# Staging the cosine chain in four slots, and spreading the token sums and splits over six pairs

## The chip, the cores and the metric

The kernel runs on one core of one Trainium2 chip. The metric is the device time of one execution in microseconds, from the first to the last of its work; the median of the runs shown is compared. TensorE is written PE here, VectorE DVE, ScalarE ACT, SyncE SP (it only issues DMAs), as in the profile.

## The reference, cut to what matters

An attention through 32 packed queries gives x (4608 tokens by 512). Two MLPs follow:

```python
def _moe_ref(x, w_gate, w_val, w_out):
    g = x @ w_gate
    silu = g * (1.0 / (1.0 + np.exp(-g)))
    return (silu * (x @ w_val)) @ w_out          # d_ff 1536

def _moe2_ref(x, w_in, w_out):                   # x: 4608 x 512
    h = x @ w_in                                 # 4608 x 2048
    g = h * np.cos(h)
    return g @ w_out                             # 4608 x 512
```

Everything is float32. The change concerns the second MLP alone: its h, its h*cos(h), and the preparation of its tokens.

## The kernel before, in words

The first half of the kernel (attention and first MLP, eight batches) writes its result to a DRAM scratch tensor. The second half, from line 625, is the second MLP. Every float32 operand of a matmul is kept as a pair (hi, lo) of float32r values, made by `split` (lines 85 to 87): ACT copies with rounding to hi, DVE subtracts to give lo. A product then takes three matmuls (hi*hi, hi*lo, lo*hi).

The second MLP works on 6 chunks of 768 tokens. In a chunk there are 8 pairs (`q`, 0 to 7; over the kernel `p`, 0 to 47), a pair being two blocks of 128 hidden features. One pair multiplies a 2x2 block of weights by a 2x2 block of tokens in Winograd's way, with seven products instead of eight. Product 0 to product 6 (`product`, lines 672 to 682) take six matmuls each into four PSUM banks A, Bk, Ck, Dk (lines 738 to 777); product 4 accumulates into A, product 5 into Ck, product 6 into Dk. Around them ACT copies A to SBUF (line 748, called p1 below), and DVE makes v = p1 + Bk, u3 = v + Ck, c22 = u3 + Dk, and later c21 and c12. c22, A, c21 and c12 are the four tiles of h of the pair (128 x 384 each).

Between the products stand up to three `down` products (lines 684 to 711), twelve matmuls of 512 columns each, that multiply finished tiles of earlier pairs by w_out. `step_down` releases those of group j (pairs 2j and 2j+1) from pair 2j+3 on, three per pair; so pairs 0 to 2 have none, and ten follow the last pair. Each result is copied or added to an SBUF accumulator by `evict`, run from the list `post`.

`chain` (lines 655 to 670) makes h*cos(h) and its split for one tile h: ACT t = h/2pi + 1/4 (line 657), ACT k = integer of t (659), DVE t = t - k (662), ACT sine of t (663), DVE t = t*h (667), ACT hi copy (86), DVE lo (87). The order of all instructions is the order in which the program issues them, and each engine takes its own in that order. The multiplication of a tile is put off to the next `chain` call (`late_mul`), the split to the one after (`late_split`), so that on ACT a call is t, k, hi copy of the tile two before, sine.

The second kind of work is the tokens of the next chunk. `load_x2` (513 to 518) loads four tiles from DRAM scratch in pair q = 3; `sums_x2` (526 to 529) makes four differences, two each at the start of q = 5 and q = 6; `split_x2` (531 to 534) splits the seven right-hand sides, all in q = 7, at seven places called by `swap_x` (742 to 744): before product 0, before v, before u3, before c22, before product 5, before product 6 and after the third of the four `chain` calls. The weights of pair p+2 are loaded by SP as the products of pair p are issued (`load_up`, fourteen buffers, 256 KB each), those for `down` two groups ahead (`load_wd`, 512 KB each). PSUM has eight banks; a pair uses four for its products and three for its downs, and each bank is handed out in the order in which banks come free. A tile gets its buffer when it is first written.

Of the kernel before, what the change touches and what calls it, by code (L numbers as in the profile page):

```python
# [10 lines left out]
F32 = mybir.dt.float32  # L11
F32R = mybir.dt.float32r
U32 = mybir.dt.uint32
I32 = mybir.dt.int32
U8 = mybir.dt.uint8
AF = mybir.ActivationFunctionType
ALU = mybir.AluOpType
# [9 lines left out]
TH = 384  # L27
NCH = NT // (2 * TH)
NPF = NF2 // 2
NG = NPF // 2  # L30
SBUFS, CBUFS = 11, 18
SIN_SCALE = 6.28318500518798828

PI = float(np.pi)
TWO_PI = 2.0 * float(np.pi)
# [5 lines left out]
def attention_mlp_kernel(ctx: ExitStack, tc: tile.TileContext, qT, kT, vP, pP, wgv, w1o, w2, out):  # L41
    nc = tc.nc
    PE, ACT, DVE, SP = nc.tensor, nc.scalar, nc.vector, nc.sync
# [37 lines left out]
    quarter = cst.tile([128, 1], F32, name="quarter")  # L81
# [3 lines left out]
    def split(src, hi, lo, eng=DVE):  # L85
        ACT.activation(out=hi, in_=src, func=AF.Copy)  # L86
        eng.tensor_tensor(out=lo, in0=src, in1=hi.bitcast(F32), op=ALU.subtract)  # L87
# [96 lines left out]
    def a_t(b):  # L184
        for r in range(2):
            e = E.pop(r)
            ET[r] = []
            for c0, n in ((0, 3), (3, 2)):
                tp = bank([128, n, 128], "tp")
                for c in range(n):  # L190
                    o = 128 * (c0 + c)
                    PE.transpose(out=tp[:, c, :], in_=e[:, o:o + 128], identity=ident)
                et = mt([128, n, 128], F32, "ET")
                ACT.activation(out=et, in_=tp, func=AF.Copy)
                ET[r].append(et)
# [20 lines left out]
    def a_ppt(b):  # L216
        for r in range(2):
            tp = bank([128, 128], "ppt")
            PE.transpose(out=tp, in_=ppu.pop(r).rearrange("p i d -> p (i d)"), identity=ident)
            ppT[b, r] = st.tile([128, 128], F32, tag="ppT", name="ppT", bufs=4)  # L220
            ACT.activation(out=ppT[b, r], in_=tp, func=AF.Copy)
# [76 lines left out]
    def flush_wo():  # L298
        while wo_wait:
            a, i, w_ = wo_wait.pop(0)  # L300
            wo[a, i] = wt([128, 2, 4, 128], F32R, "wo")
            split(w_, wo[a, i][:, 0].rearrange("p f o -> p (f o)"), wo[a, i][:, 1].rearrange("p f o -> p (f o)"))
# [10 lines left out]
    def w2_load(i):  # L313
        if i < 4 * NF2:
            w2_raw[i] = raw_words(mt, w2[i // 2, :, 256 * (i % 2):256 * (i % 2) + 256], 256)
# [44 lines left out]
    def w2_store():  # L360
        while w2_done:
            p, dst = w2_done.pop(0)
            SP.dma_start(out=dst, in_=p.bitcast(F32))
# [34 lines left out]
    def flush_split():  # L398
        while pend_split:
            pend_split.pop(0)()  # L400
# [100 lines left out]
    late = {}  # L501
# [9 lines left out]
    xb, xs = {}, {}  # L511
# [8 lines left out]
    def sum_x2(key, x, y):  # L520
        xb[key] = xt([128, 2, TH], F32, "xt")
        DVE.tensor_tensor(out=xb[key], in0=xb[x], in1=xb[y], op=ALU.subtract)

    RIGHT = ((0, 0), "t2", "t3", "t1", (1, 0), "t4", (1, 1))

    def sums_x2(n):
        sum_x2(*(("t1", (0, 1), (0, 0)), ("t2", (1, 1), "t1"), ("t3", (1, 1), (0, 1)), ("t4", (1, 0), "t2"))[n])
        if n == 2:
            del xb[0, 1]

    def split_x2(n):
        x = late["x"].tile([128, 2, 2, TH], F32R, tag="xs", name="xs", bufs=8)
        split(xb.pop(RIGHT[n]), x[:, 0], x[:, 1])
        return x

    up, wd = {}, {}

# [11 lines left out]
    with tc.manual_schedule():  # L549
# [38 lines left out]
        for b in range(B):  # L588
            g = a_up(b)
            flush_split()  # L590
            flush_wo()
            w2_store()
            if b == 0:
                w2_load(0)
            n = b + 1
            steps = {}
            if n < B:
                steps = {
                    0: (lambda: a_s1(n),),
                    2: (lambda: a_t(n),),  # L600
                    3: (lambda: a_pp(n),),
                    4: (lambda: a_ppt(n),),
                    5: (lambda: a_s2(n),),
                    6: (lambda: a_wp(n, (0, 1)),),
                }
            else:
                gates.close()
                late["x"] = ctx.enter_context(tc.tile_pool(name="xs", bufs=1, side="right", reuse_waits="tile"))
                x_now = [None] * 7
                steps = {0: (lambda: load_x2(0),)}  # L610
                for i in range(4):
                    steps[i + 1] = (lambda i=i: sums_x2(i),)

                def first_split(n):
                    x_now[n] = split_x2(n)

                for i, ns in enumerate(((0,), (3,), (2,), (1, 4), (5, 6))):
                    steps[i + 1] = steps.get(i + 1, ()) + tuple(lambda n=n: first_split(n) for n in ns)
            if b == 0:
                for i in range(4):  # L620
                    steps[i] = steps.get(i, ()) + (lambda: u_step(0, 1), lambda: u_step(1, 1), lambda: u_step(2, 1)) * 2
                steps[4] = (flush_wo,) + steps[4]
            a_down(b, g, steps)
# [4 lines left out]
        def tmp(name, dt=F32):  # L628
            return lt([128, TH], dt, "t", name, 16)
# [16 lines left out]
                load_wd(j, i)  # L646

        gs = {}
        late_mul, late_split = [], []

        def run(q, keep=0):
            while len(q) > keep:
                q.pop(0)()

        def chain(p, a, t, h_):
            t_ = tmp("t")
            ACT.activation(out=t_, in_=h_, func=AF.Identity, scale=1.0 / TWO_PI, bias=quarter)  # L657
            k_ = tmp("k", I32)
            ACT.activation(out=k_, in_=t_, func=AF.Copy)  # L659
            run(late_mul)  # L660
            run(late_split, 1)
            DVE.tensor_tensor(out=t_, in0=t_, in1=k_, op=ALU.subtract)  # L662
            ACT.activation(out=t_, in_=t_, func=AF.Sin, scale=SIN_SCALE)  # L663
            gs[p, a, t] = lt([128, 2, TH], F32R, "g", "g2", 16)

            def mul():
                DVE.tensor_tensor(out=t_, in0=t_, in1=h_, op=ALU.mult)  # L667
                late_split.append(lambda: split(t_, gs[p, a, t][:, 0, :], gs[p, a, t][:, 1, :]))

            late_mul.append(mul)  # L670

        def product(out, p, n, x, first, last):
            w = up[p, n]
# [44 lines left out]
        x_next = [None] * 7  # L718
# [7 lines left out]
        for p in range(NP_ALL):  # L726
            c, q = divmod(p, NPF)
            more = c + 1 < NCH
            if q == 0 and c:
                x_now = x_next  # L730
                x_next = [None] * 7
            if more and q == 3:
                load_x2(c + 1)
            if more and q in (5, 6):
                sums_x2(2 * (q - 5))
                sums_x2(2 * (q - 5) + 1)
            swap = more and q == NPF - 1
            full = [bank([128, TH], "p") for _ in range(4)]
            A, Bk, Ck, Dk = full
            p1, v, u3 = tmp("p1"), tmp("v"), tmp("u3")  # L740

            def swap_x(n):
                if swap:
                    x_next[n] = split_x2(n)

            swap_x(0)
            product(A, p, 0, x_now[0], True, True)
            ACT.activation(out=p1, in_=A, func=AF.Copy)  # L748
            product(Bk, p, 1, x_now[1], True, True)
            run(post)  # L750
            swap_x(1)
            DVE.tensor_tensor(out=v, in0=p1, in1=Bk, op=ALU.add)
            step_down(p)
            product(Ck, p, 2, x_now[2], True, True)
            swap_x(2)
            DVE.tensor_tensor(out=u3, in0=v, in1=Ck, op=ALU.add)
            product(Dk, p, 3, x_now[3], True, True)
            run(post)
            swap_x(3)
            c22 = tmp("c22")  # L760
            DVE.tensor_tensor(out=c22, in0=u3, in1=Dk, op=ALU.add)  # L761
            step_down(p)
            product(A, p, 4, x_now[4], False, True)
            chain(p, 1, 1, c22)
            run(post)
            swap_x(4)
            product(Ck, p, 5, x_now[5], False, True)
            chain(p, 0, 0, A)
            swap_x(5)
            product(Dk, p, 6, x_now[6], False, True)  # L770
            c21 = tmp("c21")
            DVE.tensor_tensor(out=c21, in0=v, in1=Ck, op=ALU.add)
            chain(p, 1, 0, c21)
            swap_x(6)
            step_down(p)
            c12 = tmp("c12")
            DVE.tensor_tensor(out=c12, in0=v, in1=Dk, op=ALU.add)
            chain(p, 0, 1, c12)
            if p == NP_ALL - 1:
                run(late_mul)  # L780
                run(late_split)
        while d_next < len(downs):
            step_down(NP_ALL + 2)
            run(post)
# [42 lines left out]
```

## Time and profile before

| what | value |
|---|---|
| median of 3 runs | 1560.06 us (1559.1 to 1561.91) |
| profiled execution, its own time | 1562.06 us |
| span of its profile | 1560.3 us |
| PE, DVE, ACT busy in the span | 97%, 65%, 56% |
| mean granted TensorE clock | 0.98 |
| second MLP in the span | from 744.1 us to the end |

The span runs from the first to the last instruction; the profiled execution's own time is 1.76 us longer. A row of a timeline gives the start, the duration, the engine, the line and, in square brackets, the idle time of the engine before it and what ended that. A matmul's end is modelled, so its duration is longer than its share of the stream; start-to-start distances are used for PE.

### The profile page before, as it was taken

What the parts mean: (1) busy time and instruction counts of PE and PEld (TensorE: products, weight loads), DVE (VectorE), ACT (ScalarE), POOL (GpSimd) and SP (SyncE); (2) the same over time, 40 slices, a digit from 0 to 9 for tenths busy, and PEclk for the clock granted to TensorE, in tenths of its full rate; (3) what the DMA queues carried; (4) which work ended last, traced back from release to release, by engine and by line L of the source; (5) the groups of instructions that cost most, each with busy time, mean ns of one, the idle gap of its engine ahead of it and who ended that gap; (6) DMA issues with size and microseconds to landing.
All of it is one profiled execution on the core that took longest, in us unless ns stands there. A gap on an engine that the chain in (4) does not pass through costs nothing.

```text
span 1560.3 us, 27786 instructions
## 1 busy us (share of the span) xinstructions
PE 1508.8 (97%) x10476; PEld 1361.1 (87%) x10476; DVE 1007.0 (65%) x2048; ACT 870.4 (56%) x1917; POOL 3.0 (0%) x22
## 2 busy tenths in 40 slices
PE   8999999999999999999799899899999989999999
PEld 6688989998998989999797899799889979988997
DVE  6978669394747656353457666666766666676664
ACT  6976647374655645252465555555556555655552
POOL 0000000000000000000000000000000000000000
PEclk9999999999999999999899999999999999999999
DMA  8733617164452613102765475467556547745541
GB/s 314 267 127 96 217 67 244 64 211 138 125 161 68 208 48 97 48 19 96 296 215 169 149 250 169 147 208 269 165 163 243 183 135 241 243 150 170 196 162 53
DMA packets 129414, 257.16 MB, mean 165 GB/s; under 512 B 13568, under 2 KB 37120, under 8 KB 129280
## 3 DMA queue, kind: packets, MB, share of 16 engines
q1 hardware_dynamic: 120064, 245.94, 47.2%
q10 hardware_dynamic: 9216, 9.44, 1.7%
q8 instruction: 83, 1.36, 0.3%
q14 instruction: 51, 0.42, 0.1%
HBM read 213.39 MB, written 41.94 MB: 164 GB/s over the span
## 4 chain that ended last, share of the span: by engine, by line
PE 64%; ACT 16%; DVE 12%; issue 5%; DMA 3%; SPq 0%; DVEq 0%; ACTq 0%
PE o L493 19%; PE acc L691 10%; PE p L676 9%; PE pg L433 9%; PE pv L433 9%; ACT t L657 4%; DVE t L662 4%; ACT k L659 4%; ACT g L86 3%; ACT t L663 3%; DVE g L87 3%; PE wp L386 3%; PE pg L418 1%; PE pv L418 1%; DMA up<-w2u 1%
## 5 line engine op out<-in xcount | busy, mean ns | idle before, releaser
L676 PE MATMUL p<-xs,up 128*128 128x384 f32 x2016 | 397.1, 350 | 40.2 <-ACT p L748 25.1
L676 PEld LDWEIGHTS p<-xs,up 128*128 128x128 f32 x2016 | 371.3, 197 | 58.7 <-ACT p L748 29.7
L691 PE MATMUL acc<-wd,g 128*128 128x512 f32 x1728 | 417.8, 392 | 0.0
L691 PEld LDWEIGHTS acc<-wd,g 128*128 128x128 f32 x1728 | 325.9, 190 | 58.4
L493 PEld LDWEIGHTS o<-g,wo 128*128 128x128 f32 x2304 | 307.2, 188 | 13.1 <-DVE d L250 5.9
L493 PE MATMUL o<-g,wo 128*128 128x288 f32 x2304 | 316.6, 297 | 0.0
L87 DVE TENSOR_TENSOR g<-t,g 128x384 fp32r<-128x384 f32 x192 | 107.3, 559 | 194.2 <-ACT g L86 194.0
L663 ACT ACTIVATE t<-t 128x384 f32<-128x384 f32 x192 | 101.0, 526 | 209.1 <-DVE t L662 209.1
L433 PE MATMUL pg<-a,wp 128*128 128x288 f32 x1008 | 162.4, 296 | 0.0
L433 PE MATMUL pv<-a,wp 128*128 128x288 f32 x1008 | 160.6, 294 | 0.0
L657 ACT ACTIVATE t<-c,quarter 128x384 f32<-128x384 f32 x144 | 88.9, 617 | 128.4 <-DVE c L761 113.5
L433 PEld LDWEIGHTS pg<-a,wp 128*128 128x128 f32 x1008 | 142.3, 188 | 11.7 <-ACT wp L86 8.4
L433 PEld LDWEIGHTS pv<-a,wp 128*128 128x128 f32 x1008 | 143.0, 188 | 0.0
L87 DVE TENSOR_TENSOR g<-h,g 128x288 fp32r<-128x288 f32 x192 | 87.5, 456 | 39.6 <-ACT g L86 39.4
L662 DVE TENSOR_TENSOR t<-t,k 128x384 f32<-128x384 f32 x192 | 106.0, 552 | 1.7 <-ACT k L659 1.7
L659 ACT ACTIVATE k<-t 128x384 int32<-128x384 f32 x192 | 100.8, 525 | 6.1
L441 ACT ACTIVATE silu<-pg 128x288 f32<-128x288 f32 x192 | 78.2, 407 | 42.4 <-PE pg L433 37.9
L498 ACT ACTIVATE x2e<-o 128x288 f32<-128x288 f32 x64 | 26.5, 414 | 134.6 <-PE o L493 134.6
L86 ACT ACTIVATE g<-h 128x288 fp32r<-128x288 f32 x192 | 85.0, 442 | 24.2 <-DVE h L444 23.8
L86 ACT ACTIVATE g<-t 128x384 fp32r<-128x384 f32 x192 | 97.6, 508 | 0.2 <-DVE t L667 0.2
L444 DVE TENSOR_TENSOR h<-silu,pv 128x288 f32<-128x288 f32 x192 | 86.1, 448 | 17.7 <-PE pv L433 7.4
L667 DVE TENSOR_TENSOR t<-t,c 128x384 f32<-128x384 f32 x144 | 80.1, 556 | 15.0 <-ACT t L663 9.5
(95 smaller groups left out, 1292.2 us busy)
## 6 DMA issues: line engine op xcount, KB each, us to landing
up<-w2u SPq DMA_DIRECT2D x336, 256.0 KB, 3.0
wd<-w2d SPq DMA_DIRECT2D x96, 512.0 KB, 6.2
raw<-in_w SPq DMA_DIRECT2D x64, 256.0 KB, 3.2
w2u<-w2p SPq DMA_DIRECT2D x56, 256.0 KB, 2.2
raw<-in_wgv SPq DMA_DIRECT2D x24, 512.0 KB, 7.6
vt<-in_vP SPq DMA_DIRECT2D x32, 320.0 KB, 4.2
kt<-in_kT SPq DMA_DIRECT2D x32, 288.0 KB, 5.1
qt<-in_qT SPq DMA_DIRECT2D x32, 288.0 KB, 6.2
```

The lines of the kernel that those rows point to most:

```text
L86: ACT.activation(out=hi, in_=src, func=AF.Copy)
L87: eng.tensor_tensor(out=lo, in0=src, in1=hi.bitcast(F32), op=ALU.subtract)
L433: PE.matmul(out=p_, lhsT=w[u][:, x, o:o + 128], rhs=a2[u][:, y, sl], start=(n == 0), stop=(n == 5),)
L444: DVE.tensor_tensor(out=h_, in0=s_, in1=pv, op=ALU.mult)
L493: PE.matmul(out=acc, lhsT=wo[o, f // 4][:, x, f % 4, :], rhs=g[f][:, y, sl], start=(f == 0 and i == 0), stop=(f == NF1 - 1 and i == 2),)
L657: ACT.activation(out=t_, in_=h_, func=AF.Identity, scale=1.0 / TWO_PI, bias=quarter)
L659: ACT.activation(out=k_, in_=t_, func=AF.Copy)
L662: DVE.tensor_tensor(out=t_, in0=t_, in1=k_, op=ALU.subtract)
L663: ACT.activation(out=t_, in_=t_, func=AF.Sin, scale=SIN_SCALE)
L667: DVE.tensor_tensor(out=t_, in0=t_, in1=h_, op=ALU.mult)
L676: PE.matmul(out=out, lhsT=w[:, u, 128 * k:128 * k + 128], rhs=x[:, v, k, :], start=(first and k == 0 and i == 0), stop=(last and k == 1 an ...
L691: PE.matmul(out=acc, lhsT=gs[p, a, t][:, x, o:o + 128], rhs=wd[j, f][:, y, :], start=(f == 0 and n == 0), stop=(f == 3 and n == 2),)
```

## The change

`chain` no longer runs through one tile. It appends the tile to a list and calls `slot`, which does one step for each of the last four tiles: the hi copy of the tile three before, t of the newest, DVE's subtraction and ACT's sine of the one before, k of the newest, the multiplication of the one two before, and lo of the one three before. Three empty slots end the last pair. The token loads of the next chunk move from q = 3 to the start of q = 2; its sums go one each to the starts of q = 3, 4, 5 and 6; its seven splits go one to q = 6, three to q = 7 and three to q = 0 of the next chunk (the last three being of the right-hand sides that products 4, 5 and 6 use). For the first chunk only the order in which the names of the seven split tiles are made is different.

```diff
+        def slot(new):
+            tiles.append(new)
+            n = len(tiles) - 1
+            now, one_, two, three = (at(n - i) for i in range(4))
+            if three:
+                ACT.activation(out=three["g"][:, 0, :], in_=three["t"], func=AF.Copy)
+            if now:
+                now["t"] = tmp("t")
+                ACT.activation(out=now["t"], in_=now["h"], func=AF.Identity, scale=1.0 / TWO_PI, bias=quarter)
+            if one_:
+                DVE.tensor_tensor(out=one_["t"], in0=one_["t"], in1=one_["k"], op=ALU.subtract)
+                ACT.activation(out=one_["t"], in_=one_["t"], func=AF.Sin, scale=SIN_SCALE)
+            if now:
+                now["k"] = tmp("k", I32)
+                ACT.activation(out=now["k"], in_=now["t"], func=AF.Copy)
+            if two:
+                DVE.tensor_tensor(out=two["t"], in0=two["t"], in1=two["h"], op=ALU.mult)
+            if three:
+                DVE.tensor_tensor(
+                    out=three["g"][:, 1, :], in0=three["t"], in1=three["g"][:, 0, :].bitcast(F32), op=ALU.subtract
+                )
+
         def chain(p, a, t, h_):
-            t_ = tmp("t")
-            ACT.activation(out=t_, in_=h_, func=AF.Identity, scale=1.0 / TWO_PI, bias=quarter)
-            k_ = tmp("k", I32)
-            ACT.activation(out=k_, in_=t_, func=AF.Copy)
-            run(late_mul)
-            run(late_split, 1)
-            DVE.tensor_tensor(out=t_, in0=t_, in1=k_, op=ALU.subtract)
-            ACT.activation(out=t_, in_=t_, func=AF.Sin, scale=SIN_SCALE)
             gs[p, a, t] = lt([128, 2, TH], F32R, "g", "g2", 16)
+            slot({"h": h_, "g": gs[p, a, t]})
...
-            if more and q == 3:
+            if more and q == 2:
                 load_x2(c + 1)
-            if more and q in (5, 6):
-                sums_x2(2 * (q - 5))
-                sums_x2(2 * (q - 5) + 1)
-            swap = more and q == NPF - 1
+            if more and q in (3, 4, 5, 6):
+                sums_x2(q - 3)
...
-            def swap_x(n):
-                if swap:
-                    x_next[n] = split_x2(n)
+            def swap_x(pos):
+                n = {(6, 4): 0, (7, 1): 1, (7, 3): 2, (7, 5): 3, (0, 0): 4, (0, 1): 5, (0, 2): 6}.get((q, pos))
+                if n is None or (q and not more) or (not q and not c):
+                    return
+                split_x2(n, x_next if q else x_now)
...
             if p == NP_ALL - 1:
-                run(late_mul)
-                run(late_split)
+                for _ in range(3):
+                    slot(None)
```

## Rows read from the trace of the kernel before

**Rows 1.** The page's first part: busy time, share of the span and instructions by engine.

```profile
PE 1508.8 (97%) x10476; PEld 1361.1 (87%) x10476; DVE 1007.0 (65%) x2048; ACT 870.4 (56%) x1917; POOL 3.0 (0%) x22
```

**Rows 2.** Stages: window, length, busy PE, PEld, DVE, ACT, POOL; granted clock, DMA, GB/s.

```profile
744.10:782.40 38.30, 28.96 (x140) 28.32 (x139) 20.68 (x40) 20.41 (x41) 0.00 (x0) 0.82 0.84 310
...
883.10:945.00 61.90, 61.90 (x315) 56.26 (x314) 40.44 (x78) 36.58 (x74) 0.00 (x0) 1.00 0.69 238
```

**Rows 3.** The chain of waits in order of time, two pieces one pair apart.

```profile
1030.94 3.13 PE p L676 x18
...
1046.40 3.13 PE p L676 x18
```

**Rows 4.** Timeline of PE, pairs 0 to 3: products, no downs until pair 3.

```profile
744.12 11.62 PE L676 MATMUL p<-xs,up 128*128 128x384 f32 x66
760.30 10.09 PE L676 MATMUL p<-xs,up 128*128 128x384 f32 x42 [4.56 <-ACT p L748]
775.16 7.43 PE L676 MATMUL p<-xs,up 128*128 128x384 f32 x30 [4.77 <-ACT p L748]
...
790.03 2.21 PE L676 MATMUL p<-xs,up 128*128 128x384 f32 x10
```

**Rows 5.** Timeline of PE: product 4 of pairs 23, 24 and 47, and the last downs.

```profile
1123.54 1.21 PE L676 MATMUL p<-xs,up 128*128 128x384 f32 x6
...
1146.72 2.48 PE L676 MATMUL p<-xs,up 128*128 128x384 f32 x9 [1.82 <-ACT p L748]
...
1526.22 3.29 PE L676 MATMUL p<-xs,up 128*128 128x384 f32 x18
1529.35 27.36 PE L691 MATMUL acc<-wd,g 128*128 128x512 f32 x120
```

**Rows 6.** Timeline of ACT in pair 1, from its copy p1 to the next pair's.

```profile
759.78 0.47 ACT L748 ACTIVATE p<-p 128x384 f32<-128x384 f32 x1
762.19 0.61 ACT L657 ACTIVATE t<-c,quarter 128x384 f32<-128x384 f32 x1 [1.94 <-DVE c L761]
762.84 0.52 ACT L659 ACTIVATE k<-t 128x384 int32<-128x384 f32 x1
763.27 0.51 ACT L86 ACTIVATE g<-t 128x384 fp32r<-128x384 f32 x1
764.87 0.52 ACT L663 ACTIVATE t<-t 128x384 f32<-128x384 f32 x1 [1.09 <-DVE t L662]
...
774.64 0.47 ACT L748 ACTIVATE p<-p 128x384 f32<-128x384 f32 x1
```

**Rows 7.** Timeline of DVE in pair 1, lo of one tile and the next subtraction.

```profile
763.80 0.56 DVE L87 TENSOR_TENSOR g<-t,g 128x384 fp32r<-128x384 f32 x1 [1.18 <-ACT g L86]
764.28 0.55 DVE L662 TENSOR_TENSOR t<-t,k 128x384 f32<-128x384 f32 x1
```

**Rows 8.** Groups by line: count | busy us, mean ns of one | idle before, its releaser.

```profile
L663 ACT ACTIVATE t<-t 128x384 f32<-128x384 f32 x192 | 101.0, 526 | 209.1 <-DVE t L662 209.1
L705 DVE TENSOR_TENSOR oacc<-oacc,acc 128x512 f32<-128x512 f32 x108 | 73.3, 681 | 12.1 <-PE acc L691 12.1
L87 DVE TENSOR_TENSOR xs<-xt,xs 128x768 fp32r<-128x768 f32 x24 | 22.9, 955 | 18.3 <-ACT xs L86 18.3
L86 ACT ACTIVATE xs<-xt 128x768 fp32r<-128x768 f32 x24 | 19.0, 834 | 1.6 <-ACT x2e L498 1.6
L522 DVE TENSOR_TENSOR xt<-xb 128x768 f32<-128x768 f32 x12 | 11.4, 952 | 0.0
```

**Rows 9.** The tile up from 755.3 to 755.5: pair 2's first weight load.

```profile
L541 SPq DMA_DIRECT2D up<-w2u x1: 319/319/319, 755.5 to 755.5; - x1
...
DMA to landing us min/median/max: 9.5/9.5/9.5
```

**Rows 10.** DMA from 749 to 771: what the queues moved.

```profile
DMA packets 3596, 8.65 MB, mean 393 GB/s; under 512 B 402, under 2 KB 402, under 8 KB 3594
```

**Rows 11.** The tile xb, all loads of the kernel: time from issue to landing.

```profile
DMA to landing us min/median/max: 3.5/8.6/10.0
```

More of the change, by code (lines that the diff above doesn't have):

```diff
@@ L529, in sums_x2, with new_xs, split_x2 @@
             del xb[0, 1]
[L531 to L534, printed above, removed]
+    def new_xs():
+        return late["x"].tile([128, 2, 2, TH], F32R, tag="xs", name="xs", bufs=8)
+    def split_x2(n, to):
+        if to[n] is None:
+            to[n] = new_xs()
+        split(xb.pop(RIGHT[n]), to[n][:, 0], to[n][:, 1])
     up, wd = {}, {}
@@ L608, in attention_mlp_kernel @@
                 late["x"] = ctx.enter_context(tc.tile_pool(name="xs", bufs=1, side="right", reuse_waits="tile"))
-                x_now = [None] * 7
+                x_now = [new_xs() for _ in range(7)]
                 steps = {0: (lambda: load_x2(0),)}
@@ L612, in attention_mlp_kernel @@
                     steps[i + 1] = (lambda i=i: sums_x2(i),)
-                def first_split(n):
-                    x_now[n] = split_x2(n)
                 for i, ns in enumerate(((0,), (3,), (2,), (1, 4), (5, 6))):
-                    steps[i + 1] = steps.get(i + 1, ()) + tuple(lambda n=n: first_split(n) for n in ns)
+                    steps[i + 1] = steps.get(i + 1, ()) + tuple(lambda n=n: split_x2(n, x_now) for n in ns)
             if b == 0:
@@ L648, in attention_mlp_kernel, with run, at @@
         gs = {}
-        late_mul, late_split = [], []
-        def run(q, keep=0):
-            while len(q) > keep:
+        tiles = []
+        def run(q):
+            while q:
                 q.pop(0)()
-        def chain(p, a, t, h_):
-            t_ = tmp("t")
-            ACT.activation(out=t_, in_=h_, func=AF.Identity, scale=1.0 / TWO_PI, bias=quarter)
-            k_ = tmp("k", I32)
-            ACT.activation(out=k_, in_=t_, func=AF.Copy)
-            run(late_mul)
-            run(late_split, 1)
-            DVE.tensor_tensor(out=t_, in0=t_, in1=k_, op=ALU.subtract)
-            ACT.activation(out=t_, in_=t_, func=AF.Sin, scale=SIN_SCALE)
+        def at(n):
+            return tiles[n] if 0 <= n < len(tiles) else None
+        def slot(new):
[19 more added lines that the diff above has]
+                )
+        def chain(p, a, t, h_):
             gs[p, a, t] = lt([128, 2, TH], F32R, "g", "g2", 16)
[L666 to L670, printed above, removed]
+            slot({"h": h_, "g": gs[p, a, t]})
         def product(out, p, n, x, first, last):
```

## The prediction

> **What bounds the kernel now.** I read the page's first part, then the second MLP by stages, then PE's timeline against those of ACT and DVE. PE is busy 97% of the span [rows 1], so at first sight 3% is all there is to win. The stages show where that sits: from 883 to 945 PE is busy all the time at full clock, while in the first 38 us of the second MLP it is busy 28.96 of 38.30 us at a mean clock of 0.82 [rows 2]. Busy time at half clock is loss too, so idle time alone understates it.
>
> An undisturbed pair is PE's: two pieces of the chain that start the same group of products stand 15.47 us apart, 1030.94 and 1046.40 [rows 3]. Its 42 product matmuls and 36 down matmuls are not touched by the change, so 15.46 us a pair is the floor. A product of six is then 1.04 us (3.13 for 18), and a down (15.46 - 7 x 1.04) / 3 = 2.72.
>
> From product 4 of pair 3 at 790.03 [rows 4] to product 4 of pair 47 at 1526.22 [rows 5] there are 44 pairs in 736.2 us, where 44 x 15.46 = 680.2 would do: 56.0 us are lost. They sit at the five chunk boundaries. From product 4 of pair 23 (q = 7) to that of pair 24 it takes 23.18 us [rows 5], 7.7 too many, and PE then waits for ACT's p1; five times 7.7 is 39, and the other 17 lie in the pairs next to the boundaries, where after such a wait PE runs for a while at half clock (1.2 of 2.4 GHz), as in the first stage of rows 2.
>
> Why ACT is late is seen in pair 1. Each `chain` call there leaves ACT idle 1.09 us before the sine, for DVE's subtraction; DVE in its turn has waited 1.18 us for ACT's hi copy [rows 6, 7]. Over 192 tiles the first wait alone is 209.1 us [rows 8]. With it one call takes 2.65 to 3.1 us and the loop from p1 to p1 is 774.64 - 759.78 = 14.86 us [rows 6], without downs. That is 0.6 us under PE's pair. DVE's three evictions per pair, the sums (0.95 us each) and splits (0.83 on ACT, then 0.96 on DVE behind it) [rows 8] go straight on top of such a loop.
>
> **The slot.** Seven instructions per tile stay seven. What goes is the wait inside a call: DVE's subtraction in a slot works on the k of the slot before, the hi copy on a product of the slot before. ACT's four records of a slot sum to 0.51 + 0.61 + 0.52 + 0.52 = 2.16 us [rows 6]; DVE's three to 3 x 0.56 = 1.68 [rows 7]. New waits: the hi copy waits for DVE's multiplication of the previous slot, and behind it on ACT are t, sine, k and the next p1; the subtraction waits for k of the previous slot, and behind it on DVE are evictions, v, u3, c22. The trace has no such slot, so I bound it: 1.68 (DVE's records alone) and 3.1 (the lockstep of before, nothing won). I take 2.2, nearest to ACT's records. The loop from p1 to p1 is then 2.41 (p1 to the first t [rows 6]) + 3 x 2.2 + 1.65 (t, k, sine of the last) = 10.7 us, against PE's 15.46. About 4.8 us per pair are spare; at 3.1 the loop is 14.8 and little is.
>
> **Sums and splits.** Their number and cost stay; they are now at most three splits in a pair. DVE's records in q = 7 or q = 0 are 12 x 0.56 + 5 x 0.55 + 3 x 0.68 + 3 x 0.96 = 14.4 us [rows 7, 8], under 15.46; in q = 6, one sum and one split, 13.4; in q = 3 to 5, 12.5. ACT in q = 7: 4 x 2.16 + 0.47 + 3 x 0.83 = 11.6. The loop in q = 7, each split taken in lockstep: 10.7 + 3 x 0.68 + 3 x 1.79 = 18.1, 2.6 over PE's pair, and as much again in q = 0. What covers these 5.3 us: p1's value is ready after product 0 and PE asks for the bank again at product 4, behind four products and two downs; less p1 itself that is 3 x 1.04 + 2 x 2.72 - 0.5 = 8.1 us. From q = 1 on the lag is worked off at 2.7 us per pair (15.46 - 10.7 - 2.04). So I cost this edit at nothing; without cover it is 5.3 us per boundary, 26 in all. The three splits of q = 0 stand ahead of u3, which PE wants at product 5; that is one product later than p1's bank.
>
> All 56.0 us therefore go. What is late next is nothing: PE's own stream.
>
> **The token loads.** In q = 2 they pass seven weight loads, four of w_out and up to three output stores on SP. They take 4 x 384 KB = 1.57 MB, 4.0 us at the 393 GB/s of rows 10; the passed weights are wanted two pairs, 30 us, later. They land in at most 10.0 us [rows 11] and the first sum now stands one pair, 15.46 us, after the issue. Cost nothing; if they are late, DVE waits at the head of q = 3 with v behind it, and PE at product 5, 8 us on. In pair 2 the pair is short and the DMA full; a wait there would lie between 0 and 10.0, and I take 0.
>
> **Pairs 0 to 2.** They have no downs, so PE needs 7.3 us a pair but comes every 14.9 us: it waits 4.56 and 4.77 us for p1 [rows 4]. With the slot, product 4 of pair 1 no longer waits much (p1 to p1 9 to 11 us), but then the weights of pair 2 are not there: the first is issued at 755.5 and lands 9.5 us later, at 765.0 [rows 9], behind full queues that the change does not empty [rows 10]. From 765.0 PE has seven products of pair 2 and two of pair 3 (9.4 us), then down, two products, down (7.5 us) until product 4 of pair 3: 781.9 at full clock. It will have been idle some 6 us; after idle stretches of 4.6 and 4.8 us the 42 and 30 matmuls took 10.09 and 7.43 us instead of 7.3 and 5.2 [rows 4], that is 2.2 to 2.8 more. With 2.4 product 4 of pair 3 comes at 784.3 instead of 790.03: 5.7 us won, between 5.3 and 8.1.
>
> The Trainium skill (DMA: Bandwidth & Descriptors, section Where 436 GB/s comes from) says that for transfers between HBM and SBUF the HBM side, about 358 GB/s, binds. By that the 8.65 MB of rows 10 would take 24.2 instead of 22 us and the first weight of pair 2 would come some 2 us later. The trace has 393, so the measurement decides and I keep 765.0.
>
> **What costs nothing.** A stays in its PSUM bank one slot, 2.2 us, longer: seven of eight banks are taken per pair in the order in which they come free, so that bank goes to a down of the next pair, over 6 us off; without that cover 2.2 us per pair, with a gain below zero excluded since it only frees later. The three empty slots, 6.6 us, lie behind the ten downs of 27.36 us [rows 5]; the first four (10.9 us) read older pairs. Making the seven names first moves no write.
>
> **Sum.** 56.0 + 5.7 = 61.7 us. The profiled execution's own time is 1562.06 us, 1.76 beyond the span, and becomes 1500.4. It lies 2.0 above the median of the runs, so on the median I predict 1560.06 - 61.7 = 1498.4.
>
> **Rivals.** First, the boundary keeps a wait. For it: DVE at 14.4 of 15.46 us by records, and both engines wait on each other in each split. Against: a DVE record starts before the one ahead ends, 763.80 to 764.28 for 0.56 [rows 7], so real occupation is lower. If the lag exceeds the 8.1 us cover, up to 5.3 us per boundary and a half-clock loss of 2.5 come back: 5 x 3 to 5 x 7.8, 1513 to 1537. The Trainium skill (VectorE: DVE Perf Modes, section Terms) says that the next DVE op can't issue until the pipe has emptied. By this the full 14.4 us would count and 1 us be spare; rows 7 speak against it, and my sum used the full records anyway.
>
> Second, slower: a tile is finished only when the third slot after its own runs. The third tile of an odd pair, read by the first down two pairs on, used to be done within its own pair's wake; now it needs the second slot of the next pair, which waits for products 4 and 5 there, 11.7 us in. It is wanted at 15.46 + 2.08 = 17.5. Below 5.8 us of lag nothing happens. Beyond it each of 22 odd pairs waits by the rest, and over 61.7 / 22 = 2.8 us, a lag of 8.6, the kernel is slower: at 9.5 us 22 x 3.7 = 81, 1580. The 4.8 us spare per pair speak against.
>
> Third, the change does not decouple: a slot is 3.1 us, since waits only change places. Then the loop stays 14.8, only the sums and splits are spread; half the boundary loss remains, about 1530.
>
> Fourth, DMA later than in rows 9 by the slower rate: 1500.6.
>
> **How the numbers follow.** Forecast (PE's stream throughout; 1495 to 1502, from a ramp at full clock to a remnant of 0.7 us per boundary) 0.70; boundary wait 0.15; slower 0.04; not decoupled 0.06; DMA 0.05. About 0.2%, 3 us, is what a measurement of this kernel can tell from no change; every case but the slower rival lies far beyond it on the fast side. The slower rival at a lag just over 8.6 us could also come out even, and I give that 0.02 taken from the undecoupled case: faster 0.94, same 0.02, slower 0.04. The range takes the forecast, DMA and the lower part of the boundary wait: 1494 to 1515.
>
> **What would show it.** Right: line 663's wait nearly gone; product 4 of pair 47 minus that of pair 3 at 680 to 684 us; no granted clock below 1 after some 775 us; PE's first long wait in pair 2 ended by a weight load, not by p1. Wrong: PE waits for u3 or p1 in q = 7 or 0 (first rival), for a hi or lo at the first down of odd pairs (second), or p1 to p1 in pairs 1 and 2 still over 13 us (third).

## The result and the profile after

The changed kernel takes 1501.4 us, the median of 4 runs (1499.41 to 1502.22). The kernel before, run 4 times beside it, took 1560.24 us (1559.1 to 1561.91). The ratio is 0.962, with a 95% interval from 0.9604 to 0.9637. The forecast was 1498.4 us, in a range from 1494 to 1515.

The profiled execution of the changed kernel took 1502.04 us with a span of 1500.2. The page's first part answers [rows 1]:

```profile
PE 1482.4 (99%) x10476; PEld 1343.9 (90%) x10476; DVE 985.8 (66%) x2048; ACT 839.2 (56%) x1917; POOL 3.0 (0%) x22
```

The instructions are the same in number. PE's busy time fell by 26.4 us although not one matmul went: most of that part was matmuls at half clock, since the mean granted clock rose from 0.980 to 0.995. The rest of the span's 60.1 us was idle time of PE. The stages show it (columns as in [rows 2]):

```profile
744.10:782.40 38.30, 31.32 (x165) 30.14 (x164) 23.62 (x48) 23.27 (x51) 0.00 (x0) 0.91 0.94 355
...
1300.00:1469.00 169.00, 169.00 (x855) 153.63 (x854) 113.80 (x221) 93.10 (x200) 0.00 (x0) 1.00 0.58 185
```

The second line holds nearly eleven pairs with a chunk boundary among them, and PE is busy for all of it at full clock. Only the first 38 us still have idle time and a lower clock. PE's timeline there and at the end answers [rows 4, 5]:

```profile
744.82 15.06 PE L688 MATMUL p<-xs,up 128*128 128x384 f32 x84
...
766.86 11.72 PE L688 MATMUL p<-xs,up 128*128 128x384 f32 x54 [6.98 <-DMA up<-w2u]
...
785.95 3.29 PE L688 MATMUL p<-xs,up 128*128 128x384 f32 x18
...
1466.19 3.29 PE L688 MATMUL p<-xs,up 128*128 128x384 f32 x18
1469.32 27.36 PE L703 MATMUL acc<-wd,g 128*128 128x512 f32 x120
```

The two waits for p1 in pairs 1 and 2 are gone, and one wait of 6.98 us for a weight load stands in their place. From product 4 of pair 3 to that of pair 47 it is 1466.19 - 785.95 = 680.24 us, which is 44 x 15.46 to the last digit: PE loses nothing in 44 pairs. The end (27.36 us of downs) is unchanged.

ACT in pair 1, from its copy p1 on, answers [rows 6]:

```profile
755.74 0.47 ACT L760 ACTIVATE p<-p 128x384 f32<-128x384 f32 x1
...
759.49 0.51 ACT L663 ACTIVATE g<-t 128x384 fp32r<-128x384 f32 x1
759.91 0.56 ACT L666 ACTIVATE t<-p,quarter 128x384 f32<-128x384 f32 x1
760.37 0.51 ACT L669 ACTIVATE t<-t 128x384 f32<-128x384 f32 x1
760.78 0.51 ACT L672 ACTIVATE k<-t 128x384 int32<-128x384 f32 x1
761.20 0.51 ACT L663 ACTIVATE g<-t 128x384 fp32r<-128x384 f32 x1
761.62 0.61 ACT L666 ACTIVATE t<-c,quarter 128x384 f32<-128x384 f32 x1
```

Hi copy, t, sine and k follow each other with no wait, and they belong to three tiles: t and k to the newest, the sine to the one before, the hi copy to the one three before. Over the kernel (columns as in [rows 8]), first two groups before, then three after:

```profile
L87 DVE TENSOR_TENSOR g<-t,g 128x384 fp32r<-128x384 f32 x192 | 107.3, 559 | 194.2 <-ACT g L86 194.0
...
L657 ACT ACTIVATE t<-c,quarter 128x384 f32<-128x384 f32 x144 | 88.9, 617 | 128.4 <-DVE c L761 113.5
```

```profile
L669 ACT ACTIVATE t<-t 128x384 f32<-128x384 f32 x192 | 98.2, 512 | 2.7 <-DVE t L668 2.5
...
L676 DVE TENSOR_TENSOR g<-t,g 128x384 fp32r<-128x384 f32 x192 | 106.4, 554 | 8.2 <-ACT g L663 8.0
...
L666 ACT ACTIVATE t<-c,quarter 128x384 f32<-128x384 f32 x144 | 88.5, 615 | 199.5 <-DVE c L773 193.7 <-DVE c L784 5.4
```

The sine's idle time went from 209.1 us [rows 8] to 2.7, and that ahead of DVE's lo from 194.2 to 8.2. ACT's largest wait now stands ahead of t of c22 (193.7 us, 113.5 before), and it is harmless: DVE's u3 waits for PE's products (118.9 us), c22 and t follow it. ACT now waits for the bottleneck, where before it waited for DVE inside every call.

### The profile page after: what moved, and what is told of

It reads as the page before. It is cut to its first block, busy times and chain, and to the rows that moved or that the text cites. A ratio compares the mean times of both kernels' runs of the same rounds, so it can differ in the third digit from the quotient of the medians.

```text
span 1500.2 us, 27610 instructions
## 1 busy us (share of the span) xinstructions
PE 1482.4 (99%) x10476; PEld 1343.9 (90%) x10476; DVE 985.8 (66%) x2048; ACT 839.2 (56%) x1917; POOL 3.0 (0%) x22
## 3 DMA queue, kind: packets, MB, share of 16 engines
q8 instruction: 83, 1.36, 0.4%
## 4 chain that ended last, share of the span: by engine, by line
PE 95%; DMA 3%; ACT 1%; DVE 1%; SPq 0%; issue 0%; ACTq 0%
PE acc L703 26%; PE p L688 23%; PE o L493 20%; PE pg L433 9%; PE pv L433 9%; PE wp L386 3%; PE pg L418 1%; PE pv L418 1%; DMA raw<-in_wgv 1%; DMA up<-w2u 1%; PE pp L203 1%; PE s L151 1%; PE s L229 1%; PE wp L371 0%; PE tp L192 0%; DMA vt<-in_vP 0%
## 5 line engine op out<-in xcount | busy, mean ns | idle before, releaser
L688 PE MATMUL p<-xs,up 128*128 128x384 f32 x2016 | 374.8, 338 | 7.0 <-DMA up<-w2u 7.0
L703 PEld LDWEIGHTS acc<-wd,g 128*128 128x128 f32 x1728 | 322.5, 188 | 57.1
L688 PEld LDWEIGHTS p<-xs,up 128*128 128x128 f32 x2016 | 355.9, 189 | 18.1 <-DMA up<-w2u 7.3
L666 ACT ACTIVATE t<-c,quarter 128x384 f32<-128x384 f32 x144 | 88.5, 615 | 199.5 <-DVE c L773 193.7
L433 PEld LDWEIGHTS pg<-a,wp 128*128 128x128 f32 x1008 | 142.3, 188 | 11.7 <-ACT wp L86 8.4
L768 DVE TENSOR_TENSOR u<-v,p 128x384 f32<-128x384 f32 x48 | 26.6, 554 | 119.0 <-PE p L688 118.9
L498 ACT ACTIVATE x2e<-o 128x288 f32<-128x288 f32 x64 | 26.4, 413 | 133.9 <-PE o L493 133.9
```

Of the source, the lines that this page charges most:

```text
L433: PE.matmul(out=p_, lhsT=w[u][:, x, o:o + 128], rhs=a2[u][:, y, sl], start=(n == 0), stop=(n == 5),)
L666: ACT.activation(out=now["t"], in_=now["h"], func=AF.Identity, scale=1.0 / TWO_PI, bias=quarter)
L688: PE.matmul(out=out, lhsT=w[:, u, 128 * k:128 * k + 128], rhs=x[:, v, k, :], start=(first and k == 0 and i == 0), stop=(last and k == 1 an ...
L703: PE.matmul(out=acc, lhsT=gs[p, a, t][:, x, o:o + 128], rhs=wd[j, f][:, y, :], start=(f == 0 and n == 0), stop=(f == 3 and n == 2),)
```

## The experiments

Two stretches of PE's timeline split each time. The ramp is product 0 of pair 0 to product 4 of pair 3 (45.91 us before, 41.13 after); the pairs are product 4 of pair 3 to that of pair 47 (736.19 before, 680.24 after). Each kernel ran 4 or 5 times (the kernel before with the later w_out loads 10 times), beside runs of the kernel before. In the profiles product 0 of pair 0 starts anywhere between 743.4 and 746.0 us; that spread comes from the first half, and the two stretches leave it out.

My theory was that the slots give the whole gain by decoupling ACT and DVE, that the spread sums and splits cost nothing, and that what is left in the ramp is the weights' arrival. The main rival was that the boundaries needed the spreading.

**The slots alone.** The changed kernel with loads, sums and splits where they were before:

```diff
-            if more and q == 2:
+            if more and q == 3:
                 load_x2(c + 1)
-            if more and q in (3, 4, 5, 6):
-                sums_x2(q - 3)
+            if more and q in (5, 6):
+                sums_x2(2 * (q - 5))
+                sums_x2(2 * (q - 5) + 1)
...
-                n = {(6, 4): 0, (7, 1): 1, (7, 3): 2, (7, 5): 3, (0, 0): 4, (0, 1): 5, (0, 2): 6}.get((q, pos))
...
-                split_x2(n, x_next if q else x_now)
+                if more and q == NPF - 1:
+                    split_x2(pos, x_next)
```

> The slots alone: token loads in q = 3, two sums each in q = 5 and 6, all seven splits in q = 7, as before the change. Theory (the staged chain leaves a spare of about 5 us a pair, and what q = 7 overshoots lies behind the 8.1 us between product 0 and product 4): the seven splits add 7 x 1.3 to 7 x 1.8 us to a loop of 9.7 to 10.7 plus 2.0, so 21 to 25 us against 15.46, 6 to 10 over; the boundary waits 0 to 2 us each, 1501 to 1511 us in all, and pairs 0 to 2 are as in the changed kernel. Rival (the spreading is what took the boundary waits away): at least half of the 56 us stay, 1530 or more.

It took 1501.64 us (1500.47 to 1502.73), a ratio of 0.9615 [0.9601, 0.9629]: the changed kernel's time. Ramp 41.01, pairs 680.24. PE's waits in the second MLP are the first line below (what PE waited for: us in total, times, longest); the others are product 4 of pair 8, p1 of pair 9 and product 4 of pair 9 in the timeline.

```profile
PE p L688 <- DMA up<-w2u: 7.1, 1, 7.1
```

```profile
863.94 3.29 PE L688 MATMUL p<-xs,up 128*128 128x384 f32 x18
...
871.03 0.49 ACT L759 ACTIVATE p<-p 128x384 f32<-128x384 f32 x1 [0.90 <-PE p L688]
...
879.40 3.29 PE L688 MATMUL p<-xs,up 128*128 128x384 f32 x18
```

Even with all seven splits in q = 7, PE keeps its 15.46 us across the boundary (863.94 to 879.40), and by pair 9 ACT is again the one that waits, 0.90 us for PE. The rival is refuted.

**The spread alone.** The kernel before with the changed kernel's places of loads, sums and splits (the reverse of the edit above, applied to the old `chain`).

> The spreading alone: loads in q = 2, one sum each in q = 3 to 6, splits one, three and three, but the old chain with its waits. Theory (the loop is still 15.3 us, so each sum and split is added wherever it stands and the lag only starts earlier): as before, 1553 to 1562 us, the boundary loss of about 10.5 us per chunk spread over more pairs. Rival (three splits in a pair are few enough): half of the 56 us goes, about 1530.

It took 1550.49 us (1549.0 to 1553.66), 0.9931 [0.9915, 0.9947]: 10.6 us faster than the 1561.12 beside it, where I expected less. Pairs 723.62. PE's waits, and the product behind one of them:

```profile
PE p L676 <- ACT p L748: 20.6, 7, 4.6
...
PE p L676 <- issue: 8.9, 5, 2.2
```

```profile
872.45 0.45 PE L676 MATMUL p<-xs,up 128*128 128x384 f32 x1 [2.33 <-ACT p L748]
```

The loop of 14.86 us leaves only 0.6 us of a pair of 15.46 [rows 6, 3] to work off a lag; that is how I read it that 43.4 of the 56.0 us stay (723.62 - 680.24). Spreading is worth under a fifth of the gain without slots, and nothing on top of them.

**The weights of w_out later.** For the ramp I moved the first eight w_out loads, which stand on SP's queue ahead of pair 2's weights, behind pairs 0 and 1; once on the changed kernel, once on the kernel before.

```diff
-        for j in range(2):
-            for i in range(4):
-                load_wd(j, i)
...
             chain(p, 0, 1, c12)
+            if p < 2:
+                for i in range(4):
+                    load_wd(p, i)
```

> The changed kernel, but the first two groups of w_out (4 MB) are asked for after the products of pairs 0 and 1 and not before pair 0. Theory (pairs 0 to 2 are now bound by the weights of pair 2 that queue behind those 4 MB): the 7.0 us wait for a weight is gone, the clock does not fall, and the first down of pair 3 starts near 770 us in place of 778.4; 1492 to 1497 us. Rival (the chain's latency or the clock binds there anyway): within 2 us of the changed kernel, 1499 to 1503.

> The kernel before with the same later request for the 4 MB of w_out. Theory (there pairs 0 to 2 are bound by the chain, 14.9 us from p1 to p1): no change, 1558 to 1562 us. Rival (the weights bound them there as well): some 5 us less, 1552 to 1556.

On the changed kernel 1494.55 us (1493.12 to 1495.09), 0.9569 [0.9553, 0.9585]; ramp 33.60, pairs 681.21. On the kernel before 1561.46 (1559.35 to 1564.13), 1.0001 [0.9991, 1.001]; ramp 46.30. PE in the first of the two:

```profile
743.42 19.21 PE L685 MATMUL p<-xs,up 128*128 128x384 f32 x108
...
763.95 5.70 PE L685 MATMUL p<-xs,up 128*128 128x384 f32 x30 [1.32 <-ACT p L757]
...
777.02 1.21 PE L685 MATMUL p<-xs,up 128*128 128x384 f32 x6
778.91 2.37 PE L685 MATMUL p<-xs,up 128*128 128x384 f32 x12 [0.68 <-DVE u L765]
```

The wait of 6.98 us is gone. So the order of the loads was the largest loss left in the changed kernel's second MLP, and in the kernel before the same edit was worth nothing: PE waited there mostly for p1, 29.5 us in seven waits, and for no weight. The 0.68 us before u3 is new: DVE's first sum stands ahead of v and u3, and waited for its tokens:

```profile
776.78 0.96 DVE L522 TENSOR_TENSOR xt<-xb 128x768 f32<-128x768 f32 x1 [4.23 <-DMA xb<-x2d]
```

That is the cost that I had put at 0 to 10.0 us and taken as 0. It shows only where the ramp is this short.

**A longer lag.** The fourth stage works on the tile five slots back (two more empty slots at the end):

```diff
-            now, one_, two, three = (at(n - i) for i in range(4))
+            now, one_, two, three = (at(n - i) for i in (0, 1, 2, 5))
...
-                for _ in range(3):
+                for _ in range(5):
                     slot(None)
```

> The changed kernel with the last step of a tile (hi copy and lo) two slots later still, five slots after its own. Theory (a finished tile has 5.8 us to spare before the first down of the odd pairs wants it, and a slot is 1.7 us): 2 x 1.7 = 3.4 us later costs nothing, 1500 to 1503 us. Rival (the lag of the pipeline reaches the downs): 22 odd pairs wait 1 us or more each, 1523 us or more.

1501.75 us (1500.44 to 1503.1), 0.9623 [0.9607, 0.9639]; pairs 680.24. Two slots more of lag cost nothing, so the slower rival (a down waiting for a late tile) is refuted.

**Only the order on DVE.** What is it in the slot that helps? In the kernel before, the subtraction stands on DVE behind the multiplication and lo of earlier tiles. Here it goes ahead of them; nothing else is changed:

```diff
-            run(late_mul)
-            run(late_split, 1)
             DVE.tensor_tensor(out=t_, in0=t_, in1=k_, op=ALU.subtract)
+            run(late_mul)
+            run(late_split, 1)
```

> The kernel before with one reordering on DVE alone: in a chain call the subtraction of the new tile is issued ahead of the multiplication of the tile before and of the lo of the one before that. Loads, sums and splits as before. Theory (what mattered is that on DVE the subtraction stood behind lo, which waits for ACT's hi copy; four tiles in flight are not needed): a call takes t 0.65, k 0.43, hi copy 0.43, a rest wait of 0.3 and the sine 0.43, 2.25 us, the loop 11.3 us, and the boundary waits are gone: 1500 to 1508 us. Rival (the sine must take its input from the slot before): the wait before the sine stays near 1 us, 1540 or more.

1515.38 us (1514.68 to 1515.47), 0.9706 [0.9692, 0.9721], outside the 1500 to 1508 that I expected. Pairs 691.92: two pairs of 16.7 and 16.3 at each boundary (17.87 and 16.27 at the first). The first two calls of pair 1 in the timelines of ACT and DVE, then two waits in the second MLP:

```profile
764.40 0.56 DVE L660 TENSOR_TENSOR t<-t,k 128x384 f32<-128x384 f32 x1 [1.24 <-ACT k L659]
...
766.57 0.56 DVE L660 TENSOR_TENSOR t<-t,k 128x384 f32<-128x384 f32 x1 [0.68 <-ACT k L659]
...
767.17 0.53 ACT L663 ACTIVATE t<-t 128x384 f32<-128x384 f32 x1 [0.21 <-DVE t L660]
...
767.52 0.55 DVE L87 TENSOR_TENSOR g<-t,g 128x384 fp32r<-128x384 f32 x1
767.99 0.55 DVE L772 TENSOR_TENSOR c<-v,p 128x384 f32<-128x384 f32 x1
768.57 0.62 ACT L657 ACTIVATE t<-c,quarter 128x384 f32<-128x384 f32 x1 [0.88 <-DVE c L772]
```

```profile
ACT t L663 <- DVE t L660: 41.3, 192, 0.6
...
PE p L676 <- ACT p L748: 12.0, 7, 4.2
```

The sine's wait fell from 1.09 us [rows 6] to 0.21, over all 192 tiles from 209.1 us [rows 8] to 41.3, and moving one line won 45.5 us where the changed kernel won 58.8. But DVE now waits 0.68 to 1.24 us for its own tile's k, so lo and then the next tile's sum (line 772) come late, and t waits 0.88 us for it. A part of the coupling changed places.

**The order, and lo later still.** On top of that, lo is put off to the next call, behind its subtraction:

```diff
+            DVE.tensor_tensor(out=t_, in0=t_, in1=k_, op=ALU.subtract)
+            run(late_lo)
             run(late_mul)
             run(late_split, 1)
-            DVE.tensor_tensor(out=t_, in0=t_, in1=k_, op=ALU.subtract)
...
+            def hi_then_lo():
+                ACT.activation(out=g_[:, 0, :], in_=t_, func=AF.Copy)
+                late_lo.append(lambda: DVE.tensor_tensor(out=g_[:, 1, :], in0=t_, in1=g_[:, 0, :].bitcast(F32), op=ALU.subtract))
...
```

> The run with the subtraction first, and with lo put off on DVE to the next chain call, behind that call's subtraction, so that c21 and c12 do not stand behind it either. The sine is still that of the call's own tile. Loads, sums and splits as in the kernel before. Theory (the loss was DVE's order alone; the 0.2 us before the sine does not matter): the wait of t for c21 and c12, 0.88 us in the run with the subtraction first, goes, a call takes 2.2 us, the loop 11.1 us and the boundary waits of 1.2 and 0.8 us go: 1501 to 1504 us. Rival (the sine must work on the slot before): 1510 or more.

1513.29 us (1512.72 to 1515.93), 0.9698 [0.9684, 0.9711]; pairs 690.82. A miss again: hardly better than the reordering alone (1.1 us in the pairs). Rows of a boundary suggest why (DVE and ACT, q = 7):

```profile
984.66 0.96 DVE L87 TENSOR_TENSOR xs<-xt,xs 128x768 fp32r<-128x768 f32 x1 [0.39 <-ACT xs L86]
985.53 0.55 DVE L779 TENSOR_TENSOR c<-v,p 128x384 f32<-128x384 f32 x1
986.12 0.62 ACT L657 ACTIVATE t<-c,quarter 128x384 f32<-128x384 f32 x1 [1.49 <-DVE c L779]
```

Each call still ends with the sine of its own tile, so ACT can't start a split's copy before that; DVE waits for the split, the next sum stands behind it, and ACT's next t waits 1.49 us for the sum.

**The order with the spread.** The reordering and the changed kernel's places of sums and splits, without slots.

> The run with the subtraction first on DVE (the sine still that of the call's own tile), now with loads, sums and splits spread as in the changed kernel. Theory (the slots and the spreading are two ways to the same end: either keeps PE's covers from running out, the slots by a shorter loop, the spreading by fewer splits before c22, c21 and c12 of one pair): the boundary waits go, every pair from 3 on takes 15.46 us, and 1502 to 1506 us remain for the slower pairs 0 to 2. Rival (the sine of the slot before is needed at the boundary whatever the spreading): still 1 us or more too long at each of five boundaries, 1508 to 1515.

1509.05 us (1508.03 to 1509.82), 0.9666 [0.9653, 0.968]; ramp 43.44, pairs 685.51. My forecast of 1502 to 1506 missed, the rival of 1508 to 1515 holds. Three splits now stand ahead of u3 in q = 0:

```profile
866.85 0.95 DVE L87 TENSOR_TENSOR xs<-xb,xs 128x768 fp32r<-128x768 f32 x1
867.72 0.55 DVE L756 TENSOR_TENSOR u<-v,p 128x384 f32<-128x384 f32 x1
868.37 2.35 PE L676 MATMUL p<-xs,up 128*128 128x384 f32 x12 [1.41 <-issue]
```

PE has to wait here: product 5 begins at 868.37, 0.10 us after u3's end at 868.27 (the profile calls it "issue"). So on top of the reordering the spreading does bring something, 6.4 us in the pairs (691.92 - 685.51). Without slots, the five boundaries together still lose 5.3 us (685.51 - 680.24) and the ramp 2.3.

**Each split twice.** How much room is there? The slots-alone kernel, with every split of a next chunk done a second time into the same tile, which writes the same values:

```diff
                 if more and q == NPF - 1:
+                    src = xb[RIGHT[pos]]
                     split_x2(pos, x_next)
+                    split(src, x_next[pos][:, 0], x_next[pos][:, 1])
```

> The slots alone, with every split of q = 7 done twice (the second writes the same values again). Theory (what hides the splits is the 7.9 us between p1 and product 4, of which the seven splits use 3.7): seven more splits in lockstep add 6 to 12.5 us in q = 7, so 2 to 8 us over the cover at each of five boundaries, and the clock falls after them: 1512 to 1555 us. Rival (the splits run in time that both engines have left over anyway): 1500 to 1504.

1552.73 us (1552.2 to 1553.86), 0.9947 [0.9932, 0.9962]; pairs 732.62, so each boundary costs 10.5 us ((732.62 - 680.24) / 5). PE's waits, and two places at the first boundary:

```profile
PE acc L703 <- DVE c L790: 20.1, 5, 4.2
...
PE p L688 <- DVE c L774: 12.4, 5, 2.5
```

```profile
851.09 2.29 PE L688 MATMUL p<-xs,up 128*128 128x384 f32 x6 [2.48 <-DVE c L774]
...
867.20 4.60 PE L703 MATMUL acc<-wd,g 128*128 128x512 f32 x12 [3.69 <-DVE c L790]
```

So there is a limit, as forecast, but not the one that I named. PE never waits for p1 at these boundaries: it waits for c22, which ends product 6's wait, and for c12, behind whose read a down gets its bank. These two make 32.5 of the 52.4 us in the pairs. Part of the rest is half clock: from 850.9 to 854.3 and from 867.9 to 871.3 us the granted clock was 0.5, and the down at 867.20 took 4.60 us where others take 2.88. The nearest margins are DVE's.

**Both good edits.** The slots-alone kernel with the later w_out loads, which has the token loads in q = 3 and so out of the ramp.

> The slots alone (loads in q = 3, sums in q = 5 and 6, splits all in q = 7) with the later request for the first 4 MB of w_out. In the run with the later request and the spread sums, DVE waited 4.2 us in pair 3 for the token loads of pair 2, and PE 0.7 us for u3. Theory (with the loads in q = 3 that wait goes): 1492.5 to 1494.5 us, up to 1 us under that run. Rival (the 1.3 us wait for p1 and the rest stand as they are, and loads in q = 3 only move the wait): the same within 0.5 us.

1494.77 us (1492.29 to 1495.29), 0.9572 [0.9558, 0.9586]; ramp 33.59, pairs 680.24. The wait for u3 is gone; PE's only wait left is 1.3 us for p1. The 0.97 us won in the pairs (681.21 - 680.24) is too little for the medians to show: by the time alone my forecast of 1492.5 to 1494.5 missed and the rival, the same within 0.5 us, holds. This version and the one with 1494.55 both beat both kernels, and this one does it without the spreading.

**PE kept busy through the wait.** How much of the ramp is half clock? Matmuls of zeros, whose result nothing reads, stand in the changed kernel behind pair 1, first 55 and then 26 of them:

```diff
             chain(p, 0, 1, c12)
+            if p == 1:
+                keep_busy(55)
```

> The changed kernel with 55 matmuls of a zero tile (0.11 us each, 6.1 us) after the products of pair 1, in the time in which PE waits for the weights of pair 2; their result is used by nothing. Theory (part of what pairs 0 to 2 still lose is the half clock after that wait): the clock stays full, the nine products from the first of pair 2 on take 9.4 in place of 11.6 us, and the time is 2 us less than the changed kernel's, 1498 to 1500 us. Rival (with PE faster the weights that follow are not there either, or the matmuls run into the products' time): no gain, 1500.5 to 1504.

> As the run with 55 matmuls of a zero tile in PE's wait for the weights of pair 2, but 26 of them: each came as two records of 0.11 us there, so 55 took 12.2 us and ran 4.8 us past the weights; 26 take 5.8 of the 7.0 us. Theory (half clock is 2.1 us of what pairs 0 to 2 lose, as the 54 matmuls in 9.62 us of that run in place of 11.72 suggest): the time is 2 us under the changed kernel's, 1498 to 1500.5 us, and product 4 of pair 3 starts 39 us after product 0 of pair 0 in place of 41.1. Rival (the weights after the first set the pace, not the clock): 41 us, no gain.

With 55: 1504.46 us (1503.86 to 1506.29), 0.964 [0.9627, 0.9653], ramp 44.07, slower than the changed kernel by 3, outside the 1498 to 1500 that I expected. With 26: 1500.12 (1497.7 to 1501.48), 0.9605 [0.9592, 0.9618], ramp 39.42. PE's timeline with 55, then with 26:

```profile
759.43 12.44 PE L115 MATMUL wm<-zero 128*128 128x128 f32 x110
771.62 9.62 PE L688 MATMUL p<-xs,up 128*128 128x384 f32 x54
```

```profile
760.89 5.96 PE L115 MATMUL wm<-zero 128*128 128x128 f32 x52
...
768.42 9.63 PE L688 MATMUL p<-xs,up 128*128 128x384 f32 x54 [1.56 <-DMA up<-w2u]
```

55 were too many by my own sizing: each is two records of 0.11 us, so they ran 4.8 us past the weights' arrival. But both agree on the clock: the 54 matmuls behind them took 9.62 and 9.63 us, against 11.72 after 6.98 us of idling. That makes 2.1 us of half clock, of which the shorter version's ramp got 1.7, or 1.4 against the run with the longer lag, whose ramp has the same work and took 40.77. Between 1500.12 and 1501.4 the medians can't decide; the 54 matmuls do.

## Why the prediction was right, point by point

**The 56.0 us of the boundaries.** Right: 736.19 - 680.24 = 55.95. (The pair that I read, 23.18 us, was the shortest of the five boundary pairs; the others took 24.06 to 24.09. So 42 us of the loss lay in them and not 39; the sum of 56.0 does not hang on it.) All of it comes from the slots (the slots alone give it), 44.3 of it is to be had by DVE's order alone (736.19 - 691.92). Of the other 11.7, spreading gives 6.4 without slots; the last 5.3 came with the slots alone. That it is the sine of a call's own tile which keeps splits from fitting in between is read from the rows at 984.66, and not shown: no run took that sine alone away.

**The slot.** I took 2.2 us between bounds of 1.68 and 3.1. From t at 759.91 to t at 761.62 it is 1.71; where DVE is loaded it is 1.87 (761.62 to 763.49). ACT's records of 0.51 us start 0.41 apart, so summing the records overstated it. The Trainium skill (ScalarE: Activation LUTs, section What ACT_TABLE_LOAD costs) says that back-to-back ACTIVATEs overlap by about 93 ns, and these rows, at 0.10, agree. The loop from p1 to p1 in pair 0, whose first three slots have no hi copy, was 755.74 - 746.07 = 9.67 us against my 10.7; in pair 1 the last k starts at 764.42, 8.7 us after p1. (My text's 2.65 us for a call of the kernel before stands in no row: from t to t back to back it is 3.1, the bound that I used.) The mistake had no price: PE's pair is 15.46 in any case.

**The cover of the boundary.** I let a lag of at most 5.3 us be hidden by 8.1 us between p1 and product 4. The size holds: in an undisturbed pair of the changed kernel p1 ends 7.88 us before product 4. The lag was far smaller, by my sum in part because a slot is (1.71 to 1.87 for 2.2); the rest I did not separate. At the first boundary:

```profile
860.42 0.55 DVE L768 TENSOR_TENSOR u<-v,p 128x384 f32<-128x384 f32 x1
...
861.48 0.55 DVE L773 TENSOR_TENSOR c<-u,p 128x384 f32<-128x384 f32 x1
...
863.25 3.29 PE L688 MATMUL p<-xs,up 128*128 128x384 f32 x18
...
870.34 0.49 ACT L760 ACTIVATE p<-p 128x384 f32<-128x384 f32 x1 [0.90 <-PE p L688]
```

Product 4 starts at 863.25, product 5 then 1.04 later and product 6 2.08 later. u3 ends at 860.97 and c22 at 862.03, each 3.3 us before its product. The same sum, PE's start less the end of what it needs, at a boundary of each kernel:

| kernel | p1 to product 4 | u3 to product 5 | c22 to product 6 |
|---|---|---|---|
| before, q = 7 and 0 | 0.05 | 0.05 to 0.9 | 0.06 to 1.75 |
| after, other pairs | 7.88 | 4.05 | 4.03 |
| after, q = 7 | 7.88 | 4.05 | 3.16 |
| after, q = 0 | 6.16 | 3.32 | 3.30 |
| slots alone, q = 7 | 7.87 | 4.05 | 3.16 |
| slots alone, q = 0 | 4.17 | 3.95 | 3.93 |
| each split twice, q = 7 | 6.28 | 0.05 | 0.06 |
| order and spread, q = 0 | 1.36 to 2.2 | 0.10 | 0.17 |

The boundary used 1.7 us of p1's cover (7.88 to 6.16) and 3.7 with all splits in q = 7. But u3's and c22's margins are half of p1's, and those ran out first when the splits were doubled. The step "that is one product later than p1's bank" failed as an argument: u3 and c22 are also computed later than p1, so being asked for later does not make them safer. The conclusion, no cost, held with 3 us to spare, and that was luck: of the lag that I allowed, 5.3 us, margins of 4.05 would not have covered all, and the real lag was a third of it.

**The spreading.** Its price of nothing was right. That it also brings nothing beside the slots I had not said; the three splits ahead of u3 even take its margin in q = 0 from 3.95 to 3.32.

**The ramp.** Right in mechanism: one wait, ended by pair 2's weights. Of the 5.7 us forecast 4.78 came (45.91 - 41.13), below my 5.3 to 8.1. The mis-sized term is the landing of the weights, 20.9 us after the start of pair 0 in my sum (765.0 - 744.12), 22.0 in the trace (766.86 - 744.82). They were issued a little later and took a little longer than in [rows 9], as the chain of waits shows in its piece (start, us) ahead of the 54 matmuls:

```profile
756.77 10.05 DMA up<-w2u
```

The half clock behind it was right: 2.4 forecast, 2.1 to 2.4 measured (11.72 less 9.62, or less 54 x 0.173). The full queues were as in [rows 10], at 389 GB/s:

```profile
DMA packets 3538, 8.55 MB, mean 389 GB/s; under 512 B 395, under 2 KB 395, under 8 KB 3536
```

**The 3.0 us between 1498.4 and 1501.4.** The profiled execution was forecast at 1500.4 and took 1502.04, 1.6 more: 0.9 of it is the ramp's, and 0.7 the second MLP's later start (744.82 for 744.12), which the change does not touch. The other 1.4 come from the step to the median: the profiled execution of before lay 2.0 us above its median, that of after only 0.64.

**The rivals.** The boundary wait did not come, and the spare room is known now. The slower rival is refuted by the longer lag. "Does not decouple" is refuted by line 669's 2.7 us. One sign that I had named for it did show, p1 to p1 over 13 us: from pair 1 to 2 it was 13.45 (755.74 to 769.19). But for 4.26 us of it ACT waited for PE's product, which had waited for the weight, so the sign was badly chosen. The weights came 1.2 us later than in my sum, but not by the fourth rival's slower rate: the queues moved 389 GB/s.

## What to carry to other kernels

Two in-order engines that hand one tile back and forth can be bound by the order in which each queue holds the steps, more than by their busy time, as ACT (56% busy) and DVE (65%) were here. Let each work on a tile that the other finished a step ago, before spreading load; here a new order alone gave 45 of 59 us and spreading alone 11. Then read from the timeline, for each value the bottleneck takes, how long before its use it is ready: the smallest margin, not the earliest deadline, says what breaks next, as it did when the splits were doubled. When a wait goes, look at what ends the next one (here the order of two groups of loads): an edit that was worth nothing before was worth 7 us after.

## What the runs showed of the hardware

A wait of 6.98 us of PE cost 2.1 us more behind it, since the next 54 matmuls took 11.72 us for 9.62: the granted clock was 0.50 from their start at 766.86 to 771.4 us and 1.00 behind, and 1.00 for the same matmuls in the two runs with zeros. A float32 matmul of 128x128 by 128x128 is two records of 0.11 us each, which the product's matmuls of 0.173 us for 384 columns, one record each, are not. Records on DVE overlap as those on ACT do: in the reordered kernel lo (0.55 us) starts at 767.52 and the sum behind it at 767.99, 0.47 later. What the engine does in the shared 0.08 us no run shows.
